# GpSimd drains between the last expert blocks, and the spare path's flag computed ahead of them, in an attention and mixture-of-experts kernel

## The chip, the cores and the metric

The kernel runs on one core of a Trainium2 chip. The metric is the time on the device in microseconds (us); less is better. Each time below is one execution or the median of several, as said.

## The reference

Two stages are computed one after the other, both in fp32. The first is attention of 8 batches with 8 heads, 576 positions and a head width of 64, in which each query keeps only its 32 highest scores. The second sends each of the 8 x 576 = 4608 rows (512 wide) through the one of eight experts with the highest gate score.

```python
scores = scale * np.matmul(q, k.transpose(0, 1, 3, 2))
kth = np.partition(scores, -top_k, axis=-1)[..., -top_k:-top_k + 1]
scores = np.where(scores >= kth, scores, -1000000000.0)
attn = softmax(scores)                       # written out in the reference
x = np.matmul(attn, v)                       # then laid out as (4608, 512)
...
expert_idx = np.argmax(x @ w_gate, axis=1)   # gate_w: softmax value of that expert
for e in range(E):                           # rows sorted by expert
    h = np.maximum(x_sorted[lo:hi] @ w1[e], 0.0)
    y_sorted[lo:hi] = h @ w2[e]
out = gate_w[:, None] * y
```

## The kernel before, in words

The attention works in pairs of heads and tiles of 128 queries. TensorE multiplies scores, ScalarE (ACT) evacuates and exponentiates them, VectorE (DVE) finds the 32nd highest score of each row, GpSimd (POOL) combines masks and weights. When a batch of 576 rows is finished, its rows are scattered by expert into a DRAM buffer `x_rows` with indirect transfers that GpSimd issues (L590, five for each batch). Four short transfers of blank rows follow later from GpSimd (L612), and four from SP.

The experts work in blocks of 128 rows. A block loads its rows (`load_rows`, L797) and its expert's weights (`load_weights`, L789 and L791, two transfers of 2 MB) through SP's queue. It is computed in 16 pieces (`PIECES`; `FT` is 8): 8 pieces of the first product with ReLU (L942), then 8 of the second (L959), after which ACT scales the result into `y` (L968) and `put_rows` lets GpSimd store it with an indirect transfer to `out` (L857). Between the halves a block calls `following()`, which issues the store of the block before and transposes the rows of the next. Most blocks are woven into the attention; the last ones run alone when the attention has ended: 2 plain blocks (`SURE`), 4 long blocks (`HALVES`) that carry 128 rows and another 64 of the same expert and so have two stores each, and 4 plain ones (`PLAIN`). A long block's half rows are loaded by SP at L811.

The order on TensorE, ACT and DVE inside `loop()` is the order in which the code is written. On GpSimd, `in_turn` keeps instructions in program order, and `put_rows` orders each store behind `k.last_pool`, the last instruction of the attention on that engine. `left` counts the pieces still to do, and `pieces(n)` does n of them.

Two flags decide whether a spare path runs. `rest_i` says whether blocks are left over. `any_i` says whether a row of the attention is in doubt: a DVE reduction over `doubt` into `any_p` (L1285, L1286), a 1x1 matmul into `pd` that adds over the partitions (L1288), and three small DVE operations that make `any_i` and the sum of both flags, `rare_i` (L1290, L1291, L1293). All five engines then load `rare_i` into a register (L1296) and branch over the spare path when it is 0 (L1295), as in this profile. At the end of the program stand barriers and drains that the framework writes, recorded on L1406; the opening ones are on L1397.

Of the kernel before, what the change touches and what calls it, by code (L numbers as in the profile page):

```python
# [15 lines left out]
AFTER = mybir.DependencyInfo(mybir.DependencyClass.NoSync, mybir.DependencyReason.DATA)  # L16
# [28 lines left out]
def kernel(  # L45
# [47 lines left out]
    nc = tc.nc  # L93
# [16 lines left out]
    FT = F // P  # L110
# [14 lines left out]
    HALVES = E // 2  # L125
    SURE = 2
    PLAIN = EB - upto_of[-1] - HALVES - SURE + 1
# [4 lines left out]
    k = SimpleNamespace()  # L132
# [121 lines left out]
    def in_turn(put):  # L254

        if not k.exact:
            tc.keep_in_program_order(put)
        return put
# [588 lines left out]
    def finish():  # L847
        while finishing:
            finishing.pop(0)()

    def evacuate(upto=None):

        while due and (upto is None or upto in [kind for kind, _ in due]):
            due.pop(0)[1]()

    def put_rows(x, y, rows):
        put = nc.gpsimd.indirect_dma_start(  # L857
            out=out[:, :],
            out_offset=bass.IndirectOffsetOnAxis(ap=x[0:rows, 0, Dm + 1:XW].bitcast(I32), axis=0),
            in_=y[0:rows, :], in_offset=None, bounds_check=N - 1, oob_is_err=False,  # L860
        )
        if not k.exact:
            tc.add_manual_dep(put.ins, k.last_pool.name, AFTER)

    def long_block(n, following):

# [43 lines left out]
        def last():  # L910
            for x, first, rows in ((n.x, 0, P), (n.half, P, ST)):
                py = bank("py")
                for dc in range(DT):
                    nc.tensor.transpose(py[0:rows, dc * P:(dc + 1) * P], yT[:, dc, first:first + rows], ident)
                y = k.mlp.tile([P, Dm], F32, name="y")

                def scaled(x=x, y=y, py=py, rows=rows):
                    nc.scalar.activation(
                        y[0:rows, :], py[0:rows, :], AF.Copy, scale=x[0:rows, 0, Dm:Dm + 1]
                    )  # L920
                    put_rows(x, y, rows)

                due.append(("y", scaled))
# [4 lines left out]
    def block(n, following=lambda: None, put_off=lambda store: store()):  # L928

        if not hasattr(n, "xT"):  # L930
            turned(n)
            yield "pause"
        evacuate("xT")
        hT = k.mlp.tile([P, FT, P], F32, name="hT", bufs=1)
        for half in range(2):
            while half and "y" in [kind for kind, _ in due]:
                yield "pause"
            ph = k.ps_m.tile([P, FT // 2, P], F32, name="ph", tag="m")
            for f in range(FT // 2):
                fc = half * (FT // 2) + f  # L940
                for dt in range(DT):
                    nc.tensor.matmul(  # L942
                        ph[:, f, :], n.w1[:, 0, dt, fc * P:(fc + 1) * P], n.xT[:, dt, :],
                        start=(dt == 0), stop=(dt == DT - 1),
                    )
                if f == FT // 2 - 1:
                    due.append((f"h{half}", lambda ph=ph, half=half: nc.scalar.activation(  # L947
                        hT[:, half * (FT // 2):(half + 1) * (FT // 2), :], ph, AF.Relu
                    )))
                yield  # L950
            if not half:
                finish()
        evacuate("h0")
        following()
        yield "pause"
        evacuate()
        py = bank("py") if k.apart else k.ps_m.tile([P, Dm], F32, name="py", tag="m")
        for f in range(FT):
            nc.tensor.matmul(py, hT[:, f, :], n.w2[:, 0, f, :], start=(f == 0), stop=(f == FT - 1))  # L959
            if f < FT - 1:  # L960
                yield
        y = k.mlp.tile([P, Dm], F32, name="y")

        def store():
            put_rows(n.x, y, P)

        def scaled():
            nc.scalar.activation(y, py, AF.Copy, scale=n.x[:, 0, Dm:Dm + 1])  # L968
            put_off(store)

        due.append(("y", scaled))
        yield "last"
# [5 lines left out]
    PIECES = 2 * FT  # L978
# [8 lines left out]
    with fast:  # L987
# [12 lines left out]
        left = clock = 0  # L1000
# [10 lines left out]
        def landed(n):  # L1011
            return clock is None or clock - n.at >= ON_CHIP

        def ahead():
            while waiting and len(loaded) < 2:
                expert, piece = waiting.pop(0)
                if isinstance(piece, SimpleNamespace):
                    rows_in = piece
                elif isinstance(piece, list):
                    rows_in = load_half(load_rows(SimpleNamespace(), piece[0]), piece[1])  # L1020
                elif isinstance(piece, tuple):
                    rows_in = load_rows(SimpleNamespace(), *piece, full=True)
                else:
                    rows_in = load_rows(SimpleNamespace(), piece)
                loaded.append(load_weights(rows_in, expert))
                loaded[-1].at = clock

        def put_stores():
            while stores:
                k.crowded = True  # L1030
                stores.pop(0)()
# [6 lines left out]
        def pieces(n):  # L1038
            nonlocal current, left
            while n > 0 and left > 0:  # L1040
                if current is None:
                    if not landed(loaded[0]):
                        break
                    now = loaded.pop(0)
                    if hasattr(now, "half"):
                        current = long_block(now, following)
                    else:
                        current = block(now, following, stores.append)
                    ahead()
                if clock is None:  # L1050
                    evacuate()
                step = next(current)
                if step == "pause":
                    if clock is not None:
                        break
                    continue
                if step == "last":
                    current = None
                n -= 1
                left -= 1  # L1060
            return n
# [214 lines left out]
        credit = rate = 0.0  # L1276
        with tc.manual_schedule(engines={mybir.EngineType.PE, mybir.EngineType.Activation, mybir.EngineType.DVE}):
            loop()
        pieces(left)
        finish()  # L1280
        evacuate()
        put_stores()

        any_p = k.small.tile([P, 1], F32, name="any_p")
        nc.vector.tensor_reduce(any_p, doubt, axis=AX.XYZ, op=ALU.max)  # L1285
        nc.vector.tensor_scalar(any_p, any_p, 0.0, None, ALU.is_ge)  # L1286
# [4 lines left out]
        nc.vector.tensor_tensor(rare, rare, pd[0:1, 0:1], op=ALU.add)  # L1291
        rare_i = const.tile([1, 1], I32, name="rare_i")
        nc.vector.tensor_copy(rare_i, rare)  # L1293

    with ExitStack() as outer:  # L1295
        either = nc.values_load(rare_i[0:1, 0:1], min_val=0, max_val=P + 1)  # L1296
# [114 lines left out]
```

## Time and profile before

| what | us |
|---|---|
| median of 3 runs | 1316.55 |
| lowest and highest run | 1310.98 and 1316.97 |
| the profiled execution | 1312.35 |
| its span, from the first instruction to the last | 1310.7 |
| last store issued (GpSimd, L857) | 1296.27 |
| last store landed, after its issue | 4.3 |
| the store before it: issued, landed after its issue | 1282.26, 2.7 |
| GpSimd's first closing DRAIN (L1406) | 7.021 |

Times inside the profile count from the span's start. In rows of instructions, the columns are the engine, the line and operation, how often it ran, and the shortest, median and longest duration in ns, then the first and last start in us. An engine's name with a q (POOLq, SPq, PEldq) is its sequencer, whose instructions aren't counted as busy. In a timeline row, the start and the duration in us come first, and the bracket has the idle time before the instruction and what ended it. A window's row has its length, then busy us (and instructions) of PE, PEld, DVE, ACT and POOL, then TensorE's granted clock, the busy share of the DMA engines and GB/s.

### The profile page before, as it was taken

The numbers are of one execution on the slowest core, as the hardware profiler recorded it, in microseconds if no ns is written. First come the engines' busy times: TensorE is split into PE (matmuls) and PEld (weight loads), VectorE is DVE, ScalarE is ACT, GpSimd is POOL, SyncE is SP. The second block draws the span as 40 slices with busy tenths as digits, with TensorE's granted clock in tenths as the row PEclk, the third lists the DMA queues.
The fourth block names the chain that finished last, engine by engine and source line by source line (L and its number), as shares of the span: only waits on it lengthen the run. The fifth ranks groups of instructions, "written<-read, shape, count | busy, mean of one in ns | idle before, by whom it ended". The sixth has DMA issues, their size and how long they took to land. (4 is left out here: it accounts for less than half of the span.)

```text
span 1310.7 us, 24598 instructions
## 1 busy us (share of the span) xinstructions
PE 1184.7 (90%) x7654; PEld 830.4 (63%) x7654; DVE 1064.8 (81%) x4587; ACT 931.8 (71%) x2136; POOL 715.4 (55%) x867
## 2 busy tenths in 40 slices
PE   5776676899889989999999999999999999999995
PEld 3443343666566556666666666767666777699973
DVE  7999999999999999999999999999999943000000
ACT  4888877898888888988888887898878851111210
POOL 4777766777755575658564745576558542000000
PEclk9778988999999999999999999999999999999998
DMA  5000112741474147534745554448454549986680
GB/s 150 30 30 30 31 38 90 278 165 39 142 267 137 47 158 283 175 110 159 291 174 183 161 217 174 165 149 283 147 199 158 209 161 295 386 298 213 219 286 19
DMA packets 98509, 220.95 MB, mean 169 GB/s; under 512 B 5181, under 2 KB 25917, under 8 KB 98368
## 3 DMA queue, kind: packets, MB, share of 16 engines
q1 hardware_dynamic: 91664, 199.02, 43.9%
q0 software_dynamic: 6416, 19.97, 4.3%
q8 instruction: 62, 1.02, 0.3%
q14 instruction: 79, 0.65, 0.2%
q10 hardware_dynamic: 288, 0.30, 0.1%
HBM read 195.88 MB, written 24.17 MB: 168 GB/s over the span
## 5 line engine op out<-in xcount | busy, mean ns | idle before, releaser
L418 POOL TENSOR_TENSOR w<-s,w 128x576 f32<-128x576 f32 x288 | 406.9, 1433 | 345.3 <-ACT w L409 345.2
L942 PE MATMUL ph<-xTs,w 128*128 128x128 f32 x2112 | 259.6, 276 | 3.3 <-ACT xTs L839 3.0
L942 PEld LDWEIGHTS ph<-xTs,w 128*128 128x128 f32 x2112 | 248.0, 192 | 22.5 <-issue 18.7
L959 PE MATMUL py<-w,hT 128*128 128x512 f32 x528 | 248.2, 599 | 3.6 <-ACT hT L947 3.5
L426 ACT ACTIVATE w<-w,nbias 128x576 f32<-128x576 f32 x288 | 224.1, 793 | 2.9 <-POOL w L418 2.1
L409 ACT ACTIVATE w<-s,low 128x576 f32<-128x576 f32 x288 | 207.7, 768 | 4.7
L299 PE MATMUL sc<-qkb 64*128 64x288 f32 (+1 forms) x1280 | 196.8, 459 | 9.5 <-ACT s L306 5.1
L437 PE MATMUL wTm<-turn,w 128*128 128x128 f32 x1152 | 167.7, 284 | 27.2 <-ACT oT L476 12.9
L437 PEld LDWEIGHTS wTm<-turn,w 128*128 128x128 f32 x1152 | 130.1, 144 | 84.0 <-issue 34.6
L306 ACT COPY s<-sc 128x576 f32<-128x576 f32 x288 | 168.8, 639 | 9.0 <-PE sc L299 9.0
L372 DVE MAX8 tops<-scr 128x8 f32<-128x168 f32 x576 | 165.2, 314 | 0.0
L1290 DVE CAST any_i<-pd 1x1 int32<-1x1 f32 x1 | 0.1, 147 | 201.9 <-PE pd L1288 201.9
L444 ACT COPY wT<-wTm 128x512 f32<-128x512 f32 x256 | 139.0, 603 | 23.8 <-PE wTm L437 23.7
L372 DVE MAX8 tops<-few 128x8 f32<-128x144 f32 (+1 forms) x576 | 151.0, 300 | 0.0
L299 PEld LDWEIGHTS sc<-qkb 64*128 64x128 f32 (+1 forms) x1280 | 105.4, 188 | 69.9 <-issue 32.3
L474 PE MATMUL po<-wT,vb 128*64 128x288 f32 x1024 | 148.9, 436 | 0.0
L959 PEld LDWEIGHTS py<-w,hT 128*128 128x128 f32 x528 | 91.7, 191 | 88.4 <-issue 82.7
L857 POOL DMA_INDIRECT out_dram<-y,xg x37 | 38.9, 1052 | 171.3 <-ACT y L968 86.0
L350 DVE MAX8 few<-l 128x8 f32<-128x288 f32 x288 | 126.9, 441 | 0.0
L474 PEld LDWEIGHTS po<-wT,vb 128*64 128x64 f32 x1024 | 72.1, 146 | 72.3 <-issue 22.1
L313 DVE TENSOR_TENSOR h<-s 128x576 f32<-128x576 f32 x144 | 109.1, 758 | 2.3 <-ACT s L306 2.0
L315 DVE TENSOR_TENSOR l<-s 128x576 f32<-128x576 f32 x144 | 109.0, 757 | 0.0
(190 smaller groups left out, 1701.1 us busy)
## 6 DMA issues: line engine op xcount, KB each, us to landing
w<-in_moe_w_dram SPq DMA_DIRECT2D x74, 2048.0 KB, 9.1
qkb<-in_qk_dram SPq DMA_DIRECT2D x31, 608.0 KB, 4.0
vb<-in_v_dram SPq DMA_DIRECT2D x32, 320.0 KB, 3.2
xg<-x_rows SPq DMA_DIRECT2D x37, 257.0 KB, 9.5
x_rows<-blank SPq DMA_DIRECT2D x13, 257.0 KB, 6.5
x_rows<-blank POOLq DMA_DIRECT2D x4, 257.0 KB, 9.0
x_rows<-x,posi POOLq DMA_INDIRECT x40, 3.5
out_dram<-y,xg POOLq DMA_INDIRECT x37, 4.1
```

Of the source, the lines that this page charges most:

```text
L299: nc.tensor.matmul(ps[rows, j, 0:HF], n.q[d, cols], n.k[d, keys], start=True, stop=True)
L306: lambda m=m, ps=ps: nc.scalar.copy(s[:, m, :, :], ps[:, :, 0:HF]) for m, ps in enumerate(got)
L350: nc.vector.max(out=f.few[:, m, QF + 8 * j:QF + 8 * j + 8], in_=away)
L372: nc.vector.max(out=tops[:, m, r * 8:(r + 1) * 8], in_=src[m])
L409: nc.scalar.activation(w[:, m, :], s[:, m, :, :].rearrange("p j k -> p (j k)"), AF.Relu, scale=-STEEP, bias=low[:, m:m + 1],)
L418: k.last_pool = in_turn(nc.gpsimd.tensor_tensor(w[:, m, :], s[:, m, :, :].rearrange("p j k -> p (j k)"), w[:, m, :], op=ALU.subtract)).ins
L426: nc.scalar.activation(w[:, m, :], w[:, m, :], AF.Exp, scale=scale, bias=nbias[:, m:m + 1], accum_out=n.z[:, c:c + 1])
L437: nc.tensor.transpose(pm[:, c * P:(c + 1) * P], w[:, m, first:first + P], ident)
L444: nc.scalar.copy(wT[:, :, m, q], pm4)
L474: nc.tensor.matmul(po[r, 0:HF], n.v[:, c, r], rhs, start=(c == 0), stop=(c == KC - 1))
L942: nc.tensor.matmul(ph[:, f, :], n.w1[:, 0, dt, fc * P:(fc + 1) * P], n.xT[:, dt, :], start=(dt == 0), stop=(dt == DT - 1),)
L959: nc.tensor.matmul(py, hT[:, f, :], n.w2[:, 0, f, :], start=(f == 0), stop=(f == FT - 1))
```

## The change

Three things are done. `settle()` is new: it puts a GpSimd drain into program order behind the last store issued so far, and makes later stores come behind it. The flag's computation (any_p to rare_i) moves from behind the last blocks to ahead of them. The last call `pieces(left)` is cut into three, with a `settle()` after the first and second.

```diff
@@ put_rows
         if not k.exact:
             tc.add_manual_dep(put.ins, k.last_pool.name, AFTER)
+            k.last_put = put.ins
+
+    def settle():
+        done_with = in_turn(nc.gpsimd.drain()).ins
+        tc.add_manual_dep(done_with, k.last_put.name, AFTER)
+        k.last_pool = done_with
@@ after the loop
             loop()
-        pieces(left)
-        finish()
-        evacuate()
-        put_stores()
-
         any_p = k.small.tile([P, 1], F32, name="any_p")
         nc.vector.tensor_reduce(any_p, doubt, axis=AX.XYZ, op=ALU.max)
...
         rare_i = const.tile([1, 1], I32, name="rare_i")
         nc.vector.tensor_copy(rare_i, rare)
+
+        for rest in ((HALVES + PLAIN) * PIECES - FT - 1, FT - 1):
+            pieces(left - rest)
+            settle()
+        pieces(left)
+        finish()
+        evacuate()
+        put_stores()
```

With HALVES = PLAIN = 4, PIECES = 16 and FT = 8, `rest` is 119 and 7. The first drain therefore stands 9 pieces into the first long block, behind the stores of the two SURE blocks; the second 9 pieces into the last block, behind the store of the block before it. `AFTER` is an order without a semaphore. In the built program, both drains carry no wait. GpSimd's order around them is: the store issued at 1148.70 in the profile before, drain, the eleven stores issued at 1176.48 to 1282.26, drain, the store issued at 1296.27, the load of `rare_i`.

On TensorE the built program differs in one place: the pd matmul stands ahead of the first of the last ten blocks (before the L942 matmuls at 1117.98), instead of behind the last matmul. SP's load of `rare_i` moves from behind its last weight transfer (issued at 1266.84) to ahead of the half load L811 that was issued at 1183.12. DVE, ACT and GpSimd have the rest of their instructions in the same order as before.

## The prediction

> **What bounds the kernel now.** I read the page's busy table and slices first, then the chain that ended last, then the stretches of the end by window, then the rows of the closing lines. The rows, each group from one view:
>
> ```profile
> PE 1184.7 (90%) x7654; PEld 830.4 (63%) x7654; DVE 1064.8 (81%) x4587; ACT 931.8 (71%) x2136; POOL 715.4 (55%) x867
> ...
> issue 1%; DMA 0%; POOL 0%; POOLq 0%
> ...
> 1200.00:1295.30 95.30, 95.30 (x576) 79.41 (x574) 0.00 (x0) 15.81 (x26) 7.81 (x9) 1.00 0.58 204
> ...
> 1296.00:1300.70 4.70, 0.00 (x0) 0.00 (x0) 0.00 (x0) 0.00 (x0) 0.98 (x1) 0.91 0.25 69
> 1300.70:1302.90 2.20, 0.00 (x0) 0.00 (x0) 0.00 (x0) 0.00 (x0) 0.00 (x0) 0.50 0.06 15
> 1302.90:1309.95 7.05, 0.00 (x0) 0.00 (x0) 0.00 (x0) 0.00 (x0) 0.00 (x0) 0.50 0.00 0
> ...
> 1267.81 0.98 POOL L857 DMA_INDIRECT out_dram<-y,xg  x1 [12.22 <-ACT y L968]
> 1282.26 0.98 POOL L857 DMA_INDIRECT out_dram<-y,xg  x1 [13.47 <-ACT y L968]
> 1296.27 0.98 POOL L857 DMA_INDIRECT out_dram<-y,xg  x1 [13.04 <-ACT y L968]
> ...
> L1406 POOLq DRAIN  x3: 40/109/7021, 1302.9 to 1310.5; - x3
> L1406 SPq DRAIN  x3: 7/7/13, 1303.5 to 1310.2; - x3
> L1397 POOLq DRAIN  x1: 169/169/169, 0.5 to 0.5; - x1
> L1295 POOLq INC_SWDGE_SEM  x1: 1888/1888/1888, 1301.0 to 1301.0; - x1
> L1295 PEldq COMPARE_BRANCH  x1: 3792/3792/3792, 1296.5 to 1296.5; - x1
> ...
> SPq L811 <- DMA out_dram<-y,w: 7.8, 1, 7.8
> ...
> 1117.98 7.27 PE L942 MATMUL ph<-xTs,w 128*128 128x128 f32 x63 [0.31 <-DMA w<-in_moe_w_dram]
> ...
> L1288 PE MATMUL pd<-ones,any_p x2: 163/164/164, 1295.2 to 1295.2; 128*1 128x1 f32 x2
> ```
>
> Up to 1295.3 TensorE is the bound: in the window to 1295.30 it is busy 95.30 of 95.30 us at clock 1.00. After it nothing computes, yet the span runs to 1310.7. Those 15.4 us are the tail, and the chain of waits hardly sees them: it has 1% "issue", because closing instructions are not counted as busy. The windows split the tail. 1296.0 to 1300.7: the last store is issued at 1296.27 and lands, and the engines branch over the spare path. To 1302.9: GpSimd's INC_SWDGE_SEM. To 1309.95: one GpSimd DRAIN of 7.02 us, with no engine and no transfer busy (DMA 0.00, 0 GB/s). Then 0.8 us of closing barriers. The other engines wait in the barrier for that DRAIN: SP's own drains take 7 to 13 ns and were done at 1303.6. So the tail is serial, and any us off it is a us off the kernel. Which price the DRAIN has is the whole question.
>
> **What the Trainium skill says.** "VectorE: DVE Perf Modes", section "The DRAIN you can't avoid", tells that the DRAINs of a program's preamble and postamble are constant at about 12 ns on all five engines. The trace agrees on ACT, DVE, PE and SP (7 to 17 ns) and not on GpSimd, where the first closing one takes 7,021 ns; the measurement decides. "Perfetto Trace Analysis", section "DMA Instruction — SWDGE (GPSIMD)", says a GpSimd transfer's row ends when the descriptors are written, not when the data moved; the trace agrees (rows of 0.98 us, landing 2.7 us after the issue at 1282.26). "DMA: Bandwidth & Descriptors", section "SWDGE vs HWDGE vs iDMA", says that GpSimd cores write such transfers' descriptors into rings in SBUF; that something must be taken back from these rings is my inference, stated nowhere. "Runtime: NRT & Kernel Launch", section "Instruction fetch mechanics", says a taken branch to a target outside the window costs a DMA fetch; the trace agrees (a 3.79 us branch on PE, and 10 packets on the instruction queues between 1296 and 1303).
>
> **Part 1: the closing DRAIN.** Four GpSimd DRAINs are in the trace: 0.17 us at the start, before any transfer; 7.02 us at the end, after 85 transfers of its own (40 of L590, 37 + 4 of L857, 4 of L612); then 0.11 and 0.04 us with nothing new between. So the price needs transfers, and no transfer was moving while it was paid. Two readings fit. By number: 7,021 / 85 = 83 ns for each transfer since the last drain. Fixed: about 7 us whenever anything was sent. In the changed order, the first new drain stands behind the store of 1148.70, the second behind that of 1282.26, and one transfer is left for the closing DRAIN. By number it then costs 0.08 us over the empty 0.04 to 0.17, so I take 0.17: a gain of 7.02 - 0.17 = 6.85 us. Bounds: 0 (fixed) and 6.98 (empty drain of 0.04). I take the number because all drains with nothing behind them are cheap and no transfer was in flight, so what is left is bookkeeping on GpSimd, which should grow with what is booked. What is late next: SP's barrier arrival at 1303.6, if it still came then, would cap the gain at 6.3; SP gets there earlier by part 3.
>
> **Part 2: the two new drains.** By number the first covers 73 transfers (85 less 12 stores that follow 1148.70), 73 x 83 ns = 6.1 us. Behind it on GpSimd stands only the store of 1176.48, 26.8 us idle before. Even waiting for the landing of the 1148.70 store (6.1 us) it ends near 1161: cost 0. The second covers 11 transfers, 0.9 us, behind the landing at 1284.96; its follower is the last store, which waits on ACT until 1296.0. The cover is 1296.27 - 1283.24 = 13.0 us; even at the fixed price it would end at 1284.96 + 7.02 = 1292.0. Cost 0; if the cover were gone, each us over 13.0 would delay the last store by one.
>
> **Part 3: the flag.** The pd matmul (2 passes, 2 x 0.164 us) and three DVE operations (0.147 + 0.132 + 0.142) move from 1295.2 to behind the expert block that ends near 1117.7. There TensorE waits 0.31 us for weights before its next matmul, as the row at 1117.98 shows, which hides the roughly 0.2 us of overlapped pd passes; if it does not, the loss is 0.2, at most 0.95 with the 0.76 us issue gap seen before pd at the end. I take 0.1. DVE is idle there (201.9 us of idle before L1290). PE's next transpose waits for DVE's read of pd, but comes a half block, 7 us, later. SP's load of the flag with its register work (0.27 + 0.16 + 0.02, about 0.5 us) now stands ahead of a half-load L811 and, behind it, the weights and rows of the last blocks. It reaches that place near 1175.1, 57 us after the flag is ready, and then waits 7.8 us for a store to land anyway: cost 0. In return the flag's 0.6 us after the last matmul leaves PE, DVE and SP; GpSimd gains none, since its flag load stood behind the last store's wait on ACT (until 1296.0, the flag being there at 1295.81). But SP and DVE can now branch long before the end, and PE about 1 us earlier, so their instruction fetches no longer fall onto the last store. That store took 4.34 us to land, the one before 2.70: up to 1.64 us are to be had, and GpSimd waits for exactly this landing (1300.61) before INC_SWDGE_SEM. ACT's and GpSimd's own fetches stay. I take half, 0.8; bounds 0 and 1.64. INC_SWDGE_SEM's 1.89 us: a fetch packet runs inside it, so I leave it; bounds of its change 0 and 1.86 (0.027 at the start).
>
> **Sum**, against the profiled execution (1312.35 us, of which the span is 1310.7 and 1.65 lie around it): -6.85 - 0.8 + 0.1 = -7.55, so 1304.8 there. The runs shown spread from 1310.98 to 1316.97 with the median at 1316.55, so the profiled execution was among the quick ones. On the median the forecast is 1316.55 - 7.55 = 1309.0 us, 0.57% less.
>
> **Rivals.** (B) The DRAIN's price is fixed: one late transfer is enough to pay 7.02 again, the two earlier ones are hidden, and only part 3 remains: 1316.55 - 0.7 = 1315.9. For it: a single 7 us figure cannot tell fixed from proportional, and polling a fixed set of rings would look the same. Against: three cheap drains. (C) Half and half, about 3.5 us fixed and the rest by number: 1316.55 - 3.4 - 0.7 = 1312.4. Nothing in the trace favours it. (D) Slower: the second drain holds GpSimd past 1296.0, when y is ready. It decides from 13.0 us on; if it took 20 us, because a drain behind a store in flight is much dearer than the closing one, the last store goes out 7 us late, and with an unchanged closing DRAIN the time is 1316.55 + 7 = 1323.5. For it: no drain with a store in flight is in the trace. Against: the closing price for all 85 is 7.02. (E) The drains do not do what they say, standing elsewhere on GpSimd than behind those stores: they carry no semaphore waits, but the order of the built program has them there; I count it within B.
>
> **How the numbers follow.** A 0.60, B 0.26, C 0.06, D 0.08. The measurement can tell about 0.5% of this kernel, 6.6 us, from no change. A stands at 7.55, just over it: with half a per cent between the runs, I count three quarters of A as faster, 0.45, and 0.15 as same; of B 0.03 faster, 0.21 same, 0.02 slower; of C 0.02 faster, 0.04 same; D is slower. Together faster 0.50, same 0.40, slower 0.10. Range: low is the quickest run less A's larger gain, 1310.98 - 6.98 - 1.64 = 1302.4; high is B on the slowest run with nothing gained, 1317.0, and a little: 1317.5. A alone on these runs: 1302.4 to 1311.
>
> **What would show it.** Right: a GpSimd DRAIN under 0.3 us as the first closing one, one of about 6 us near 1150, one of 1 to 3 us near 1283, the last store still issued about 1.0 us after the last matmul, and the span near 1303. Landing of the last store nearer 2.7 than 4.3 confirms the fetches; SP's and DVE's branches long before 1296 are their cause. Wrong: a closing DRAIN still near 7 us (B), a last store with idle before it put down to GpSimd's queue (D), or a new PE wait near 1118 on DVE or near 1176 behind SP's flag load.

## The result, and the profile after

| | before | changed |
|---|---|---|
| median of 8 runs, us | 1311.38 | 1303.66 |
| lowest and highest, us | 1309.14 to 1316.97 | 1302.20 to 1307.21 |
| profiled execution, us | 1312.35 | 1302.84 |
| its span, us | 1310.7 | 1301.2 |

The ratio is 0.9932 with a 95% interval of 0.9916 to 0.9948, which is 8.9 us of 1311.38 (6.8 to 11.0); the two medians differ by 7.7 us. The median of before was 1316.55 in its first three runs, two of which lay high; of these eight it is 1311.38, and of the 8 to 27 runs of before taken beside the experiments it lay between 1313.05 and 1313.67. The change is faster, and the forecast of 7.55 us lies inside the interval.

The stretches of the end in the changed kernel, by window, with columns as in the windows shown of before:

```profile
1200.00:1295.10 95.10, 95.08 (x573) 79.13 (x571) 0.00 (x0) 15.81 (x26) 7.65 (x8) 1.00 0.57 203
1296.00:1299.40 3.40, 0.00 (x0) 0.00 (x0) 0.00 (x0) 0.00 (x0) 0.98 (x1) 0.84 0.22 83
1299.40:1299.70 0.30, 0.00 (x0) 0.00 (x0) 0.00 (x0) 0.00 (x0) 0.00 (x0) 0.50 0.00 0
1299.70:1300.45 0.75, 0.00 (x0) 0.00 (x0) 0.00 (x0) 0.00 (x0) 0.00 (x0) 0.50 0.03 11
1300.45:1301.20 0.75, 0.00 (x0) 0.00 (x0) 0.00 (x0) 0.00 (x0) 0.00 (x0) 0.50 0.00 0
```

TensorE is as full as before until the last matmul (95.08 of 95.10 us). The rest is a tail of 6.1 us, where it was 15.4. The landing stretch (the second row) is 1.3 us shorter than before's 4.7, the stretch of INC_SWDGE_SEM has shrunk from 2.2 to 0.3, and the 7.05 us of the DRAIN to 0.75, of which most is no longer the DRAIN, as the next rows show.

These are the rows of the two new drains (L867), of the closing lines (L1415, before L1406) and of the branch over the spare path with the instructions just behind it (L1304, before L1295), in ns and us:

```profile
L867 POOLq DRAIN  x2: 3416/6368/9320, 1148.3 to 1281.8; - x2
...
L1415 POOLq DRAIN  x3: 52/109/131, 1299.7 to 1301.0; - x3
L1415 SPq DRAIN  x3: 7/7/13, 1300.4 to 1300.7; - x3
...
L1304 POOLq EVENT_SEMAPHORE  x6: 17/30/43, 1298.9 to 1299.4; - x6
...
L1304 DVEq COMPARE_BRANCH  x1: 72/72/72, 1118.9 to 1118.9; - x1
L1304 SPq COMPARE_BRANCH  x1: 53/53/53, 1267.1 to 1267.1; - x1
L1304 PEldq COMPARE_BRANCH  x1: 3488/3488/3488, 1289.5 to 1289.5; - x1
L1304 ACTq COMPARE_BRANCH  x1: 50/50/50, 1295.7 to 1295.7; - x1
L1304 POOLq COMPARE_BRANCH  x1: 58/58/58, 1296.2 to 1296.2; - x1
L1304 POOLq INC_SWDGE_SEM  x1: 195/195/195, 1299.5 to 1299.5; - x1
```

The longest closing DRAIN on GpSimd is 0.131 us instead of 7.021. INC_SWDGE_SEM fell too, from 1.888 to 0.195. DVE, SP and PE branch at 1118.9, 1267.1 and 1289.5; before, all five engines branched between 1296.4 and 1296.5. These are the rows of before for the other four engines (PE's stands with the prediction) and for GpSimd's first closing instructions:

```profile
L1295 POOLq EVENT_SEMAPHORE  x6: 17/30/43, 1300.4 to 1300.9; - x6
...
L1295 ACTq COMPARE_BRANCH  x1: 50/50/50, 1296.4 to 1296.4; - x1
L1295 POOLq COMPARE_BRANCH  x1: 58/58/58, 1296.4 to 1296.4; - x1
L1295 SPq COMPARE_BRANCH  x1: 53/53/53, 1296.4 to 1296.4; - x1
...
L1295 DVEq COMPARE_BRANCH  x1: 72/72/72, 1296.5 to 1296.5; - x1
```

GpSimd's first closing instruction comes 3.91 us after the end of its branch before, and 2.64 us after it in the changed kernel.

The last matmul ends at a slightly different time in each execution, so the tails are best compared from the issue of the last store (1296.274 before, 1296.085 after) to the end of the span. The steps are read from GpSimd's own instruction records.

| step on GpSimd | before | after | difference |
|---|---|---|---|
| store issued, to past its wait for the landing | 4.36 | 3.06 | -1.31 |
| the other waits, to INC_SWDGE_SEM | 0.33 | 0.33 | 0 |
| INC_SWDGE_SEM, to the DRAIN's start | 1.92 | 0.23 | -1.69 |
| DRAIN | 7.02 | 0.13 | -6.89 |
| from its end to past the barrier (SP's arrival) | 0.05 | 0.62 | +0.57 |
| the barriers behind it | 0.80 | 0.79 | 0 |
| sum | 14.47 | 5.15 | -9.32 |

The two spans differ by 9.5 us; the remaining 0.2 is the earlier end of the matmuls. What ended the first step is not the same in both. Before, the store landed 4.34 us after its issue, about 0.07 us after GpSimd could have passed its wait (the wait came 0.17 us behind the instruction ahead of it, where that is 0.10 in the changed kernel). In the changed kernel it landed after 2.74 us, and GpSimd itself came to the wait only at 3.06.

The new drains hide: this is GpSimd's timeline at their followers.

```profile
1148.51 0.98 POOL L857 DMA_INDIRECT out_dram<-y,xg  x1 [14.06 <-ACT y L974]
1176.29 0.98 POOL L857 DMA_INDIRECT out_dram<-y,xg  x1 [26.81 <-ACT y L924]
...
1282.07 0.98 POOL L857 DMA_INDIRECT out_dram<-y,xg  x1 [13.47 <-ACT y L974]
1296.09 0.98 POOL L857 DMA_INDIRECT out_dram<-y,xg  x1 [13.04 <-ACT y L974]
```

Both stores that follow a drain still wait for ACT's result, with the same 26.81 and 13.04 us of idle time as before.

### The profile page after: what moved, and what is told of

Its sections match the earlier page's. It is cut to its first block, busy times and chain, and to the rows that moved or that the text cites. A ratio compares the mean times of both kernels' runs of the same rounds, so it can differ in the third digit from the quotient of the medians.

```text
span 1301.2 us, 24599 instructions
## 1 busy us (share of the span) xinstructions
PE 1188.8 (91%) x7654; PEld 832.2 (64%) x7654; DVE 1064.4 (82%) x4587; ACT 931.3 (72%) x2136; POOL 717.2 (55%) x867
## 5 line engine op out<-in xcount | busy, mean ns | idle before, releaser
L474 PE MATMUL po<-wT,vb 128*64 128x288 f32 x1024 | 153.0, 446 | 0.0
L350 DVE MAX8 few<-hl 128x8 f32<-128x72 f32 x576 | 99.2, 210 | 0.0
```

Of the source, the lines that this page charges most:

```text
L350: nc.vector.max(out=f.few[:, m, QF + 8 * j:QF + 8 * j + 8], in_=away)
L474: nc.tensor.matmul(po[r, 0:HF], n.v[:, c, r], rhs, start=(c == 0), stop=(c == KC - 1))
```

## The experiments

In the theory called "by number", a GpSimd DRAIN pays for each transfer that GpSimd issued since the last drain. Its rivals are that the price is paid once by the first drain, that it depends on rows, or on the place among the closing instructions. A second question came from the profile after: whether INC_SWDGE_SEM shrank through the drains or through the flag.

Kernels are edits of the changed kernel. In the rows of lines shown below, L867 is the added drain, and the closing lines have other numbers in each kernel; the times of a row are lowest, median and highest in ns, then the first and the last start in us. In GpSimd's timeline the columns are start and duration in us, the instruction, and in brackets the idle time before it with what ended it.

**1. The flag alone.**

```diff
-        for rest in ((HALVES + PLAIN) * PIECES - FT - 1, FT - 1):
-            pieces(left - rest)
-            settle()
         pieces(left)
```

> The flag ahead of the last blocks, no new drains. By number of transfers: the closing GpSimd DRAIN still has 85 transfers behind it and takes 7.0 us. The last store lands about 2.7 us after its issue (it was 4.3), because SP, DVE and PE fetch their closing instructions earlier. INC_SWDGE_SEM: if its 1.89 us were a wait for instruction fetch, it falls to about 0.2 and the kernel gains 1.3 + 1.7 = 3.0 us (ratio to before 0.998); if they were bookkeeping that the new drains do earlier, it stays at 1.9 and the gain is 1.3 us (0.999).

Measured: ratio 0.9994 (0.9986 to 1.0002). The rows of the closing lines in this kernel:

```profile
L1412 POOLq DRAIN  x3: 40/109/7021, 1305.4 to 1313.0; - x3
...
L1301 POOLq INC_SWDGE_SEM  x1: 1888/1888/1888, 1303.5 to 1303.5; - x1
```

Both prices are those of before to the nanosecond. So the early flag shrinks neither. That INC_SWDGE_SEM waits for an instruction fetch becomes unlikely here, and experiment 2 refutes it, where the fetches come as before and INC_SWDGE_SEM is short. From the last store's issue to the end this kernel takes 13.12 us, 1.35 less than before. As a share of the run that is 0.1%, inside the interval, which alone can't tell it from nothing.

**2. The drains alone.** The block from any_p to rare_i stays behind put_stores(), as before.

```diff
+        for rest in ((HALVES + PLAIN) * PIECES - FT - 1, FT - 1):
+            pieces(left - rest)
+            settle()
         pieces(left)
         finish()
         evacuate()
         put_stores()
 
         any_p = k.small.tile([P, 1], F32, name="any_p")
...
```

(The diff is against the kernel before.)

> Both new drains, the flag behind the last matmul as before. By number: closing DRAIN 0.13 us. The last store lands 4.3 us after its issue, as before, since all five engines branch and fetch at 1296. SP, whose closing steps ended at 1303.6 before, caps the gain: 6.3 us, ratio 0.995. INC_SWDGE_SEM: fetch theory 1.9 us, bookkeeping theory 0.2 us. If the flag's move were needed for the drains to help, the time would be as before (1.000).

Measured: ratio 0.9937 (0.9923 to 0.9951). The rows of its closing lines:

```profile
L1415 POOLq DRAIN  x3: 52/109/131, 1300.6 to 1301.9; - x3
L1415 SPq DRAIN  x3: 7/7/13, 1301.3 to 1301.6; - x3
...
L1304 POOLq INC_SWDGE_SEM  x1: 195/195/195, 1300.4 to 1300.4; - x1
```

The drains shorten both prices. The tail is 6.44 us, 8.03 less than before, not 6.3: SP was expected to arrive at 1303.6 as before and cap the gain, and it arrived at 1301.3. In every one of these profiles SP's arrival comes 0.66 us after GpSimd's DRAIN starts (1302.885 and 1303.544 before, 1300.633 and 1301.295 here). SP's last steps begin within 0.06 us of the end of GpSimd's INC_SWDGE_SEM in every profile, and move with it (1302.798 and 1302.854 before, 1300.549 and 1300.598 here). The two halves add up: 1.35 + 8.03 = 9.38 against 9.32 for both.

The DMA queues between 1296 and 1303 bear on the flag's 1.35 us. The columns are packets, MB and the share of the 16 engines' time in the window. First this kernel:

```profile
q0 software_dynamic: 80, 0.26, 13.3%
q14 instruction: 8, 0.07, 3.7%
q8 instruction: 2, 0.03, 2.2%
```

Then the changed one:

```profile
q0 software_dynamic: 80, 0.26, 9.8%
q14 instruction: 4, 0.03, 1.4%
```

With the late flag, where five engines branch together, there are ten instruction packets, five ahead of and among the store's 80 and five behind them; with the early flag four are left. The store takes more engine time with the late flag (13.3% against 9.8% of seven microseconds), and it lands 4.19 us after its issue, against 2.74 in the changed kernel (at 1298.82). But the landing is not the whole of it. From the end of its branch to its first closing instruction GpSimd takes 3.94 us here, and between 2.51 and 2.80 in every kernel with the early flag. Here the store had landed 0.15 us before GpSimd passed the wait for it. The early flag thus shortens two things that end almost together, the store's landing and GpSimd's way to its closing instructions, and the gain needs both. That the instruction packets delay them is read from these counts; no run tests it by itself.

**3. The second drain alone.**

```diff
-        for rest in ((HALVES + PLAIN) * PIECES - FT - 1, FT - 1):
+        for rest in (FT - 1,):
```

> Only the drain in the last block, the flag early. By number of transfers: this drain has 84 transfers behind it, so it takes about 7.0 us beyond the landing of the store in flight or beside it, between 8 and 10 us in all, ends before the last store is due 13.0 us after, and the closing DRAIN takes 0.13 us; the time is that of the changed kernel (0.993). If a long drain held the last store, the store's idle time would end on GpSimd's own queue, and the time would be above the changed kernel's.

Measured: ratio 0.9930 (0.9917 to 0.9943), the changed kernel's value. The row of its one new drain:

```profile
L867 POOLq DRAIN  x1: 8159/8159/8159, 1285.3 to 1285.3; - x1
```

and the last store in its GpSimd timeline:

```profile
1299.56 0.98 POOL L857 DMA_INDIRECT out_dram<-y,xg  x1 [13.04 <-ACT y L974]
```

One drain for 84 transfers ends 6.95 us after the row of the store ahead of it (1286.52 to 1293.47), and the last store still waits for ACT. The first of the two drains in the change is not needed for the time.

**4. The first drain alone.**

```diff
-        for rest in ((HALVES + PLAIN) * PIECES - FT - 1, FT - 1):
+        for rest in ((HALVES + PLAIN) * PIECES - FT - 1,):
```

> Only the drain behind the store near 1148, the flag early. By number: 12 transfers are left for the closing DRAIN, 12 x 0.083 = 1.0 us, of which SP's closing steps hide about 0.6. If the price is one that only the first drain after any transfers pays: closing DRAIN 0.13 us.

Measured: one execution of 1306.00 us. The rows of the closing lines:

```profile
L1415 POOLq DRAIN  x3: 52/109/1039, 1302.5 to 1304.1; - x3
...
L1304 POOLq INC_SWDGE_SEM  x1: 420/420/420, 1302.1 to 1302.1; - x1
```

Twelve transfers left, 1.039 us. A price that only the first drain pays is refuted. The tail is 5.72 us, 0.57 more than the changed kernel's.

**5. A drain in the middle of the attention.** The two drains at the end are left out; the flag stays early.

```diff
                 put_stores()
                 scatter(1)
+                if i == 82:
+                    settle()
```

> One drain early in the attention, behind 29 of the 85 transfers, the flag early. By number of transfers: this drain costs 29 x 0.083 = 2.4 us beside the landing of what is in flight, and the closing DRAIN, with 56 left, 4.6 us. If only the first drain pays: about 7 us there and 0.13 us at the close.

Measured: one execution of 1308.24 us. The rows of the closing lines, then of the new drain:

```profile
L1414 POOLq DRAIN  x3: 52/109/4649, 1301.1 to 1306.3; - x3
...
L867 POOLq DRAIN  x1: 6376/6376/6376, 607.7 to 607.7; - x1
```

GpSimd's timeline behind that drain:

```profile
614.17 0.22 POOL L378 TENSOR_SCALAR nbias<-tops 128x2 f32<-128x2 f32 x1 [3.06 <-PE ph L948]
```

The closing price for 56 transfers is as expected. The drain itself lasted 6.4 us, of which 2.4 were expected for its 29 transfers; its row begins at 607.7 beside GpSimd work that ends only at 611.1, with the landing of a scatter behind it. The timeline shows what it costs where GpSimd is in use: 3.06 us idle before the next operation. The wait named there, on PE, was not the cause: the drain ends at 614.06.

**6. More transfers, hardly more rows.** Each store is followed by a transfer of 8 rows into a spare buffer.

```diff
             k.last_put = put.ins
+            r = slice(k.copied * FT, (k.copied + 1) * FT)
+            more = nc.gpsimd.dma_start(copies[r, :], y[0:FT, :]).ins
+            tc.add_manual_dep(more, put.ins.name, AFTER)
+            k.copied += 1
```

(with `copies` a DRAM tile, and no new drains)

> No new drains, the flag early; each of the 41 stores is followed by one more transfer of 8 rows from GpSimd into a spare buffer in DRAM, work that the reference does not have. By number of transfers: 126 x 0.083 = 10.4 us for the closing DRAIN. By rows or descriptors moved (10,112 rows before, 328 more): 7.2 us. Paid once whatever was sent: 7.0 us.

Measured: one execution of 1319.91 us. The rows of the closing lines:

```profile
L1418 POOLq DRAIN  x3: 40/109/10369, 1307.1 to 1318.1; - x3
...
L1307 POOLq INC_SWDGE_SEM  x1: 2716/2716/2716, 1304.4 to 1304.4; - x1
```

41 more transfers with 3% more rows raise the price by 3.35 us. It goes by transfers, not by rows, and not by their form: indirect and plain ones count alike.

**7. The drains with nothing in flight.** Both wait for a ReLU that runs long after the store ahead of them has landed (`last_h` is kept from the ReLUs of `block` and `long_block`).

```diff
         tc.add_manual_dep(done_with, k.last_put.name, AFTER)
+        tc.add_manual_dep(done_with, k.last_h.name, WAIT)
```

> Both new drains wait for the ReLU of the second half of their block, so that no transfer is in flight when they start. By number: the first takes 73 x 0.083 = 6.1 us, the second 11 x 0.083 = 0.9 us, the closing one 0.13 us, and the time is that of the changed kernel (ratio 0.993). If the 9.3 and 3.4 us of the changed kernel's drains were bookkeeping and not waiting for a landing, they stay at 9.3 and 3.4.

Measured: ratio 0.9937 (0.9918 to 0.9957). The row of the two new drains:

```profile
L867 POOLq DRAIN  x2: 946/3494/6041, 1161.3 to 1291.4; - x2
```

6.041 us for 73 transfers and 0.946 for 11: the rest of the changed kernel's 9.3 and 3.4 us was the store's row and its landing.

**8. A drain that nothing hides.** It waits for the ScalarE result of the last block, as the last store does, and stands ahead of that store (`last_y` is kept from L974).

```diff
-        for rest in ((HALVES + PLAIN) * PIECES - FT - 1, FT - 1):
-            pieces(left - rest)
-            settle()
         pieces(left)
         finish()
         evacuate()
+        settle()
         put_stores()
...
+        tc.add_manual_dep(done_with, k.last_y.name, WAIT)
```

> One drain, waiting for the same ScalarE result as the last store and standing ahead of it, the flag early: nothing hides it. By number: it takes 84 x 0.082 + 0.06 = 6.9 us with nothing in flight, the last store goes out 6.9 us later, near 1303 where it was near 1296, INC_SWDGE_SEM and closing DRAIN stay at 0.2 and 0.13 us. Of the 9.3 us that the changed kernel saves behind the last matmul, 9.3 - 6.9 = 2.4 are left: ratio 0.998. If it is the drain's place among the closing instructions that makes it dear, and not its number, the drain is short here and the time is near the changed kernel's 0.993.

Measured: ratio 0.9985 (0.9978 to 0.9993). The row of the drain:

```profile
L867 POOLq DRAIN  x1: 6939/6939/6939, 1297.2 to 1297.2; - x1
```

and the last store in GpSimd's timeline:

```profile
1305.04 0.98 POOL L857 DMA_INDIRECT out_dram<-y,xg  x1 [20.62 <-issue]
```

The price is the same at another place, so it isn't a matter of the closing instructions. It now holds the last store, whose 20.62 us of idle time are 13.0 + 6.9 and the drain's own start and end. What remains of the gain is 0.15%, 2.0 us, where 2.4 were expected.

**The two prices together.** Each DRAIN here ran with nothing in flight; INC_SWDGE_SEM stands ahead of the closing one.

| transfers since the last drain | DRAIN, us | INC_SWDGE_SEM, us | kernel |
|---|---|---|---|
| 1 | 0.131 | 0.195 | changed |
| 11 | 0.946 | | 7 |
| 12 | 1.039 | 0.420 | 4 |
| 56 | 4.649 | 1.308 | 5 |
| 73 | 6.041 | | 7 |
| 84 | 6.939 | | 8 |
| 85 | 7.021 | 1.888 | before, 1 |
| 126 | 10.369 | 2.716 | 6 |

Through the rows of 12 and 126, the DRAIN costs (10.369 - 1.039) / 114 = 0.082 us a transfer and 0.06 besides; every other row lies within 0.02 of that line. INC_SWDGE_SEM costs (2.716 - 0.195) / 125 = 0.020 us a transfer and 0.175 besides. Together each undrained transfer costs 0.102 us at the end.

## Why the prediction was right, and where it was not

The time of 1303.66 lies in the range, and the likeliest case was the one that happened. The forecast point of 1309.0 stood 5.3 us above it, which is almost wholly the base: 1316.55 was the median of three runs, two of which lay high. The saving is the better test: 7.55 us forecast, 8.9 measured (6.8 to 11.0), 9.32 in the tails of the profiles. The largest term was right in size and cause. The others together came out 1.7 us too small. That the two medians differ by 7.7 us, so close to 7.55, is luck.

- **Part 1, the closing DRAIN:** 6.85 us forecast, 6.89 found. The 83 ns for each transfer, divided out of a single row, were 82, and the choice of number over a fixed price is shown by experiments 4, 6 and 8. What a drain does for each transfer, and so the prediction's idea of taking something back from the rings, no run shows.
- **What is late next:** SP's arrival was said to cap the gain at 6.3 us unless SP came earlier through the flag. It comes earlier, but because it moves with GpSimd's INC_SWDGE_SEM (experiment 2). Its last steps still cost 0.57 us that had been hidden under the DRAIN and that the sum left out.
- **INC_SWDGE_SEM:** left unchanged for the packet of instructions that ran inside it, with 1.86 as the outer bound. This is the step that failed. It is a second price by number, and falls by 1.69 us with the drains; experiments 1 and 2 separate it from the flag. The coincidence of a packet was taken for a cause.
- **Part 3, the fetches:** 0.8 us taken between 0 and 1.64, 1.31 found. The store lands 1.6 us sooner, as forecast, but the prediction took the landing as all that GpSimd waits for, and GpSimd's own fetch as unchanged. Before, GpSimd's own closing instructions came almost as late as the landing. Had they kept their 3.91 us behind the branch, a sooner landing alone would have gained about 0.07 us (an estimate from the rows above). They fell to 2.64, and GpSimd passes the wait at 1299.14, 0.3 us after the landing. The half that the sum took was a guess between bounds.
- **Part 2, the new drains:** hidden as forecast. Their rows are longer than the 6.1 and 0.9 us forecast for the bookkeeping, since a row begins while the store ahead is still issuing and holds until that store has landed; experiment 7 finds 6.04 and 0.95 without it. They stand where the order of the built program has them, so rival E falls too.
- **Rivals:** the fixed price (B) and the half and half (C) are refuted by the line through eight rows. The slower case (D) has a mechanism that exists, as experiment 8 shows, but its point of decision, 13.0 us, was never near.

What is left is **part 3, the pd matmul**, at 0.1 us. The timeline of PE in the changed kernel shows it in the place of the wait for weights:

```profile
1117.63 0.19 PE L1289 MATMUL pd<-ones,any_p 128*1 128x1 f32 x2
1117.75 7.41 PE L948 MATMUL ph<-xTs,w 128*128 128x128 f32 x64
```

The 0.31 us of idle time before the next matmul are gone, so it cost nothing. SP's flag load cost nothing either: the half load behind it still waited 7.1 us for its store.

## What to carry to other kernels

A tail in which no engine computes is worth reading instruction by instruction: the busy table and the chain of waits count it as next to nothing, and here it was 15.4 us long. Count GpSimd's own transfers, and put a drain where GpSimd is idle anyway, late enough to leave few transfers behind it and early enough to end before its next instruction is due; one was enough here (experiment 3). Where an instruction's cost has two explanations that both fit a single profile, vary the count before trusting either.

## What the runs showed of the hardware that was not expected

INC_SWDGE_SEM, which looks like a semaphore operation, costs 20 ns for each undrained GpSimd transfer. A drain also seems to do about half of its work only after the last transfer has landed: behind the last packet of the store in flight, the changed kernel's drains ran another 3.50 us with 73 transfers and 0.84 us with 11, a slope of 43 ns where the whole price is 82; for the 29 transfers of experiment 5 that gives 0.84 + 18 x 0.043 = 1.61 us, and 1.59 was found. The drain of experiment 3, with 84 transfers, does not lie on this line: it ran 5.59 us behind the store's last packet where the line gives 3.98. It ended 6.95 us after the store's row, which is the whole price without a wait; half of that, 3.5 us, is longer than the 1.36 us until the last packet, so it can be fitted to the reading, but doesn't support it. The reading was not tested by itself and stays open.
